# Read-and-gate kernel on one core: products of states and w_in for two slices at a time, state reads written in pairs, and the slots of the attention steps set anew

## The chip, the cores and the metric

The kernel runs on one core of one Trainium2 chip. The metric is the device time of one execution in microseconds (us). Of 13 runs of the kernel before, the median is 235.89 us (235.24 to 241.19). One execution was also recorded by the hardware profiler. Its trace gives the start and the length of every instruction and of every transfer; the page sums it up.

The names of the engines are those of the profile: PE is TensorE's matmuls, PEld its weight loads, DVE is VectorE, ACT is ScalarE, POOL is GpSimd, SP is SyncE, which here only issues transfers.

## What is computed

There are 8 batches of 8 heads with 512 tokens x and 32 states each, 64 wide. Tokens read from states and states read from tokens, both by softmax attention. The 544 rows of a batch (512 token reads, then 32 state reads, all heads side by side, 512 columns) go through a two-layer network of inner width 2048 with the activation "snake". From the reference:

```python
scores = scale * np.matmul(x, state.transpose(0, 1, 3, 2))   # a: softmax over the states
xread = np.matmul(a, state)
scores2 = scale * np.matmul(state, x.transpose(0, 1, 3, 2))  # a2: softmax over the tokens
sread = np.matmul(a2, x)
...
h = x @ w_in
s = np.sin(alpha * h)
g = h + s * s / (alpha + 1e-09)
return (g @ w_out).astype(np.float32)
```

The output has 8 × 544 = 4352 rows of 512 f32.

## The kernel before

**Two halves.** The large part is the network. The 4096 token rows are worked as 8 row tiles of 512, one for each batch (t = 0 to 7), and the 8 × 32 = 256 state rows are a ninth tile (t = 8). The inner width 2048 is worked in 16 slots f of 128 columns. So the main loop has 9 × 16 slots, and slot numbers in the tables count on through the tiles.

**One slot.** mm1(t,f) (L380) makes a 128x512 tile of h transposed in a "h" tile of PSUM (4 buffers), with two matmuls (L385). For token rows the product is not states times attention and then w_in: the states of the batch are multiplied with w_in first, which gives M (L353, m_step), and mm1 multiplies M with the attention AT. For the last tile mm1 takes w_in and the state reads xs_all directly (L391). ScalarE makes the sine (L397). Its square is made by POOL (L402) or, for the slots in table SQ, by VectorE (L409). Two slots later VectorE makes gT = h + square / alpha (L412, snake), which frees the h tile. Last come matmuls of mm2 (L421): each adds one 128-wide slice of gT times w_out to a 128x512 output tile in an "o" tile of PSUM (2 buffers). How many of them a slot has is in the tables TWO0, TWO1 and TWO, counted over the 64 of the row tile before (4 row groups of 128 rows, 16 slices each). A finished row group is copied by ScalarE (L427) and stored by SyncE (L433).

**The attention of the next batches** is put between by the table BATCH, in slots counted from the start of the tile before the batch's own ("P", "T", "S", "X", "R", "N", "A", "L") or from its own start ("W", "M"). Entry 3 holds for batches 3 to 7. The steps of a batch:

- L: POOL issues the load of x (L143; f32 in memory, bf16 on chip), through the same queue in which it computes its squares.
- P: two copies of VectorE pack x by token and head (L239, xp).
- T: transpose of xp, by TensorE and a VectorE copy for batches 0 and 1, from batch 2 by one transposing transfer that SyncE issues (L260).
- S: scores, two groups g of eight small matmuls (L276), into a "px" tile of PSUM each (2 buffers). X: the exponent on ScalarE (L285), which frees it; before it and after it ScalarE loads another table.
- R: sums and reciprocals (L289, L290); N: normalizing (L297 for g = 0, L300 for g = 1), on VectorE for the g in table ND, otherwise on POOL; A: transpose of the attention, AT, from batch 2 by a transfer (L266).
- W, Cs: the state reads and their sums over the tokens (L321, L332). Then xs: a reciprocal (L341) and two multiplications (L344) write the 32 state reads of the batch into xs_all.
- M: m_step (L353), one for each of four 512-column slices of w_in: eight matmuls of 32 columns in the array (L366, 64*32 in the profile) into two px tiles, then two copies to SBUF, each on ScalarE (L375) or VectorE (L377) as MA says.

**xs_all** is [P, Q, Ns, B]: for a head pair q and a state j the 8 batches lie next to each other. One batch writes single bf16 elements 16 bytes apart.

**What sets the order.** The schedule is written out by hand: the order of instructions on each engine is that in which the loop issues them, and a slot does its steps in this order:

```python
cur = mm1(t, f)
for fn, args in pe.get(t * FT + f, []): fn(*args)      # T, S, W, Cs, AT_, m_step
pend.append((t, f) + cur)
if len(pend) > LAG: snake(*pend.pop(0))                # LAG = 2
if due: squares()
for args in two.get(t * FT + f, []): mm2(*args)
for fn, args in post.get(t * FT + f, []): fn(*args)    # L, P, T_dma, X, R, N, AT_dma, xs
```

An instruction that waits holds up all behind it on its engine. SyncE's queue holds the stores and the transposing transfers; POOL's the loads of x and of the weights (L166 w_in, L169 w_out, in the order LOADS) beside its squares and normalizing.

**Start and end.** Before the loop, batch 0 is loaded, transposed and scored, with dummy matmuls between (warm_up, table WARM). After the loop the two row groups of the last tile are multiplied and stored; mm2_last (L440) does the second in halves.

Of the kernel before, what the change touches and what calls it, by code (L numbers as in the profile page):

```python
# [12 lines left out]
BF16 = mybir.dt.bfloat16  # L13
FP32 = mybir.dt.float32
# [5 lines left out]

BATCH = {0: {'M': (-11, 0, 6, 8), 'MA': ((1, 0), (1, 1), (1, 0), (1, 1))},
 1: {'P': (0, 1),
     'T': (3, 3),
     'S': (3, 3),
     'X': (3, 3),
     'R': (3, 7),
     'N': (8, 10),
     'A': 13,  # L30
     'M': (-6, 0, 3, 9),
     'MA': ((1, 1), (1, 1), (1, 1), (0, 1)),
     'W': (5, 5)},
 2: {'L': -8,
     'P': (-1, -1),
     'T': 1,
     'S': (6, 6),
     'X': (6, 6),
     'R': (7, 8),
     'N': (7, 11),  # L40
     'A': 11,
     'M': (-5, -2, 5, 10),
     'MA': ((1, 1), (1, 1), (1, 1), (0, 1)),
     'W': (-1, -1)},
 3: {'L': -18,
     'P': (-12, -11),
     'T': -6,
     'S': (2, 2),
     'X': (2, 2),
     'R': (3, 4),  # L50
     'N': (3, 9),
     'A': 12,
     'M': (-3, 1, 6, 8),
     'MA': ((1, 0), (1, 0), (0, 1), (1, 1)),
     'W': (-2, -2)}}

SQ = {0: (4, 8, 9, 11, 12, 15),
 1: (3, 6, 11, 12, 14),
 2: (0, 2, 5, 10, 11, 14),
 7: (0, 1, 2, 3, 4, 5, 8, 10, 12),  # L60
 8: (0, 1, 2, 3, 4, 8, 9, 11, 12, 14)}
ND = {1: (), 2: (0,), 3: (0,)}
XS0 = 0

TWO0 = (0, 0, 0, 0, 0, 4, 3, 1, 0, 0, 1, 6, 1, 2, 3, 0)
TWO1 = (2, 4, 2, 1, 1, 2, 3, 2, 5, 3, 9, 3, 0, 3, 3, 0)
TWO = (7, 3, 4, 7, 0, 6, 11, 5, 4, 1, 0, 6, 2, 4, 1, 3)
WARM = (9, 2, 1, 1)
LATER = 6

LOADS = ('i0', 'i1', 'x1', 'i2', 'o0', 'o1', 'i3', 'o2', 'o3')


@with_exitstack
def kernel(
# [9 lines left out]
    nc = tc.nc  # L85

    B, H, S, D = x.shape
    Ns = state.shape[2]
    P = nc.NUM_PARTITIONS
    C = S // P  # L90
    Q = H // 2
    G = 2
    HH = H // G
    TB = S + Ns
    DFF = moe_w_in.shape[1]
    FT = DFF // P
    FS = 4
    FW = DFF // FS
# [3 lines left out]
    const = ctx.enter_context(tc.tile_pool(name="const", bufs=1))  # L102
# [10 lines left out]
    psH = ctx.enter_context(tc.tile_pool(name="psH", bufs=4, space=bass.MemoryType.PSUM))  # L113
    psO = ctx.enter_context(tc.tile_pool(name="psO", bufs=2, space=bass.MemoryType.PSUM))
    psX = ctx.enter_context(tc.tile_pool(name="psX", bufs=2, space=bass.MemoryType.PSUM))
# [39 lines left out]
    w_in_sb = wpool.tile([P, Q, DFF], BF16, name="w_in_sb")  # L155
# [24 lines left out]
    stT = const.tile([P, B * G, P], BF16, name="stT")  # L180
    nc.vector.memset(stT[:].bitcast(U32), 0)
    alpha_sb = const.tile([P, FT], FP32, name="alpha_sb")
    inva_sb = const.tile([P, FT], FP32, name="inva_sb")
    xs_all = const.tile([P, Q, Ns, B], BF16, name="xs_all")

    def warm_up(n):
        if n:
            wp = psO.tile([P, S], FP32, name="o_ps", tag="o")
        for _ in range(n):
            nc.tensor.matmul(wp[:], warm[:, 0:P], warm[:], start=True, stop=True)  # L190
# [32 lines left out]
    class Att:  # L223
# [81 lines left out]
                    ALU.mult,  # L305
                )

        def AT_(a, gs, copy=nc.vector.tensor_copy):
            tp = psX.tile([P, len(gs), S], BF16, name="a_ps", tag="px")
            for k, g in enumerate(gs):  # L310
                for i in range(C):
                    nc.tensor.transpose(
                        tp[:, k, i * P:(i + 1) * P], a.A[:, g, i], ident[:]
                    )
            copy(a.AT[:, gs[0]:gs[-1] + 1, :], tp[:])

        def W(a, pool=psX, tag="px"):
            a.wc = pool.tile([P, Q, 3 * Ns], FP32, name="w_ps", tag=tag)
# [20 lines left out]
        def xs(a):  # L339
            rC = smallp.tile([P, Q, Ns], FP32, name="rC")  # L340
            nc.vector.reciprocal(rC[:], a.wc[:, :, 2 * Ns:])  # L341
            for r in range(2):
                rows = slice(r * D, (r + 1) * D)
                nc.vector.tensor_tensor(  # L344
                    xs_all[rows, :, :, a.b],
                    a.wc[rows, :, r * Ns:(r + 1) * Ns],
                    rC[rows],
                    ALU.mult,
                )

    def m_step(b, fs, on_act):  # L353
        if fs == 0:
            Ms[b] = mpool.tile([P, G, DFF], BF16, name="M")
        if b == 0 and fs == 0:
            mp = [psH.tile([P, FW], FP32, name="m0_ps", tag="h") for _ in range(G)]
        else:
            mp = [psX.tile([P, FW], FP32, name="m_ps", tag="px") for _ in range(G)]
        for h in range(2):  # L360
            for g in range(G):
                for r in range(2):
                    rows = slice(r * D, (r + 1) * D)
                    c0 = h * 2 * Ns + r * Ns
                    o0 = h * 2 * Ns + (r ^ g) * Ns
                    nc.tensor.matmul(  # L366
                        mp[g][o0:o0 + Ns, :],
                        stT[rows, b * G + g, c0:c0 + Ns],
                        w_in_sb[rows, 2 * g + h, fs * FW:(fs + 1) * FW],
                        start=True, stop=True,  # L370
                    )
        for g in range(G):
            dst = Ms[b][:, g, fs * FW:(fs + 1) * FW]
            if on_act[g]:
                nc.scalar.copy(dst, mp[g][:])  # L375
            else:
                nc.vector.tensor_copy(dst, mp[g][:])  # L377


    def mm1(t, f):  # L380
        n = S if t < B else B * Ns
        hp = psH.tile([P, S], FP32, name="h_ps", tag="h")
        if t < B:
            for g in range(G):
                nc.tensor.matmul(  # L385
                    hp[:, :n], Ms[t][:, g, f * P:(f + 1) * P], atts[t].AT[:, g, :],
                    start=(g == 0), stop=(g == G - 1),
                )
        else:
            for q in range(Q):  # L390
                nc.tensor.matmul(  # L391
                    hp[:, :n], w_in_sb[:, q, f * P:(f + 1) * P],
                    xs_all[:, q].rearrange("p j b -> p (j b)"),
                    start=(q == 0), stop=(q == Q - 1),
                )
        s = sinp.tile([P, S], BF16, name="s")
        nc.scalar.activation(s[:, :n], hp[:, :n], ACT.Sin, scale=alpha_sb[:, f:f + 1])  # L397
        s2 = sinp.tile([P, S], BF16, name="s2")
        if f in SQ[kind(t)]:
            late.append((s2, s, n))  # L400
        else:
            nc.gpsimd.tensor_tensor(s2[:, :n], s[:, :n], s[:, :n], ALU.mult)  # L402
        return hp, s2, n
# [26 lines left out]
    def store(t, st, o_sb, cols, eng):  # L430
        if t < B:
            r0 = t * TB + st
            eng.dma_start(out[r0:r0 + C * (P - 1) + 1:C, cols], o_sb[:, cols])  # L433
        else:
            r0 = S + st * P // B
            ov = out.rearrange("(b t) c -> t b c", t=TB)
            eng.dma_start(ov[r0:r0 + P // B, :, cols], o_sb[:, cols])


    def mm2_last(t, st):  # L440
# [23 lines left out]
    a = atts[0] = Att(0)  # L464
# [13 lines left out]
        load(*w)  # L478
    a.Rs(1)
    a.N(1, nc.vector)  # L480
    m_step(0, 0, (True, True))
    a.W(psO, "o")
    a.Cs()
    warm_up(WARM[3])
    nc.scalar.activation(tiny[:, 1:2], warm[:, 0:1], ACT.Sin)
    a.AT_([0], nc.scalar.copy)
    a.AT_([1])
    nc.vector.tensor_scalar(inva_sb[:], alpha_sb[:], 1e-9, None, op0=ALU.add)
    nc.vector.reciprocal(inva_sb[:], inva_sb[:])
# [5 lines left out]
    def add(d, s, fn, *args):  # L495
        d.setdefault(s, []).append((fn, args))
# [8 lines left out]
    for b in range(B):  # L505
        p = BATCH[min(b, 3)]
        s0 = (b - 1) * FT
        if b > 1:
            add(post, s0 + p["L"], load_x, b, 1)
        if b:  # L510
            add(post, s0 + p["P"][0], first, b)
            for g in range(G):
                add(post, s0 + p["P"][g], att, b, "pack", g)
            if b == 1:
                for g in range(G):
                    add(pe, s0 + p["T"][g], att, b, "T", g)
            else:
                add(post, s0 + p["T"], att, b, "T_dma")
            for g in range(G):
                add(pe, s0 + p["S"][g], att, b, "S", g)  # L520
                add(post, s0 + p["X"][g], att, b, "X", g)
                add(post, s0 + p["R"][g], att, b, "Rs", g)
                eng = nc.vector if g in ND[min(b, 3)] else nc.gpsimd
                add(post, s0 + p["N"][g], att, b, "N", g, eng)
            if b == 1:
                add(pe, s0 + p["A"], att, b, "AT_", [0, 1])
            else:
                add(post, s0 + p["A"], att, b, "AT_dma")
        s0 = b * FT
        if b:  # L530
            add(pe, s0 + p["W"][0], att, b, "W")
            add(pe, s0 + p["W"][1], att, b, "Cs")
        add(post, s0 + (p["W"][1] if b else XS0), att, b, "xs")
        for k in range(0 if b else 1, FS):
            add(pe, s0 + p["M"][k], m_step, b, k, p["MA"][k])

    def rows(t, counts, todo):
        for f, c in enumerate(counts):
# [65 lines left out]
```

## Time and profile before

| | |
|---|---|
| median of 13 runs | 235.89 us |
| the profiled execution | 235.61 us |
| its span, first to last instruction | 233.8 us |
| mean granted TensorE clock | 0.993 |
| instructions | 4190 |
| VectorE copies of M (L377) | x18, 685 ns each |
| ScalarE copies of M (L375) | x46, 590 ns each |
| products of states and w_in (L366) | x256 matmuls, 64*32 |
| stores (L433, L437) | x35, 2.2 to 2.3 us to landing |
| transposing transfers of x and of A | x6 and x6, 3.9 and 3.0 us to landing |

Of the 235.61 us some 1.8 lie around the span. In the lists of groups, a row has the line, the engine, the operation, the tiles out<-in, the shapes, how often it occurs, then busy time and mean duration, then the idle time of the engine just ahead of it and what ended that. In a timeline, a row has the start, the duration, and in brackets how long the engine was idle before, with the releaser. Matmuls overlap in the array, so the busy times of rows in TensorE's timeline overlap at their edges; a 128x512 matmul's own record is longer than the time by which it moves the stream on.

Where x's tiles come from and when: x of batch 1 was issued at 6.94 us and took 10.17 to land, that of batch 2 was issued at 28.94 and took 7.44.

### The profile page before, as it was taken

The page shows a single profiled execution, that of the slowest core. Times are in us where ns is not written, and L with a number is a line of the kernel's source. Part 1 is how long each engine was busy: PE and PEld are TensorE (multiplying, and loading weights), DVE is VectorE, ACT ScalarE, POOL GpSimd, SP SyncE. Part 2 cuts the span into 40 slices and gives each one's busy share as a digit, 9 for nine tenths or more (in the row PEclk, how much of TensorE's full clock was granted, in tenths as well). Part 3 has the DMA queues.
Part 4 walks back from the last instruction along what each step waited for, and adds up shares of the span by engine and source line. Part 5 has one row for each costly group of instructions (what it writes and reads, how often), then busy time and mean ns, then how long its engine had stood idle before and what let it go on. Part 6 is the DMA issues. An engine that isn't in the chain of part 4 may idle for free.

```text
span 233.8 us, 4190 instructions
## 1 busy us (share of the span) xinstructions
PE 219.3 (94%) x1534; PEld 103.4 (44%) x1534; DVE 184.0 (79%) x314; ACT 163.6 (70%) x265; POOL 109.0 (47%) x116
## 2 busy tenths in 40 slices
PE   7767897799999999999999999999998999999993
PEld 3524242444544444444444443444444434565652
DVE  3779898998996999879996999699959976654500
ACT  4787975997696769775978597859776666544420
POOL 3875777446336732674167417641565033512110
PEclk9997999999999999999999999999999999999999
DMA  6999998607811780278026912440212011111113
GB/s 222 193 197 206 206 142 107 171 3 181 135 45 47 179 135 3 90 178 133 7 91 90 182 45 93 110 114 4 90 45 77 15 49 62 72 46 46 45 48 90
DMA packets 36613, 23.35 MB, mean 100 GB/s; under 512 B 19680, under 2 KB 32240, under 8 KB 36592
## 3 DMA queue, kind: packets, MB, share of 16 engines
q0 software_dynamic: 11504, 7.87, 23.9%
q1 hardware_dynamic: 25056, 15.21, 22.2%
q8 instruction: 12, 0.20, 0.3%
q14 instruction: 9, 0.07, 0.1%
q10 hardware_dynamic: 32, 0.01, 0.0%
HBM read 17.31 MB, written 8.91 MB: 112 GB/s over the span
## 4 chain that ended last, share of the span: by engine, by line
PE 72%; DMA 12%; DVE 7%; POOL 3%; issue 2%; ACT 2%; ACTq 0%; POOLq 0%
PE o_ps L421 44%; PE h_ps L385 18%; DMA xnat<-in_x_dram 8%; PE m_ps L366 3%; PE h_ps L391 3%; DVE gT L412 2%; DVE xs_all L344 2%; PE s_ps L276 2%; DMA st_nat<-in_state_dram 2%; POOL s L402 1%; DMA AT<-A 1%; DMA out_dram<-o_sb 1%; DVE rC L341 1%; DVE xp L239 1%; PE w_ps L321 1%
## 5 line engine op out<-in xcount | busy, mean ns | idle before, releaser
L402 POOL TENSOR_TENSOR s<-s 128x512 bf16<-128x512 bf16 (+1 forms) x84 | 85.8, 1027 | 109.6 <-ACT s L397 104.7
L421 PE MATMUL o_ps<-w_out_sb,gT 128*128 128x512 bf16 x528 | 134.9, 380 | 0.0
L397 ACT ACTIVATE s<-h_ps,alpha_sb 128x512 bf16<-128x512 f32 (+1 forms) x144 | 93.7, 669 | 52.0 <-PE h_ps L385 37.0
L412 DVE SCALAR_TENSOR_TENSOR gT<-s,inva_sb,h_ps 128x512 bf16<-128x512 bf16 (+1 forms) x144 | 99.4, 712 | 20.9 <-POOL s L402 19.7
L385 PE MATMUL h_ps<-AT,M 128*128 128x512 bf16 x256 | 75.0, 383 | 3.6 <-DVE gT L412 2.3
L421 PEld LDWEIGHTS <-gT 128*128 128x128 bf16 x528 | 49.1, 98 | 57.4 <-issue 6.9
L385 PEld LDWEIGHTS <-M 128*128 128x128 bf16 x256 | 24.7, 98 | 34.9 <-issue 7.9
L409 DVE TENSOR_TENSOR s<-s 128x512 bf16<-128x512 bf16 (+1 forms) x60 | 25.2, 429 | 6.5 <-ACT s L397 5.9
L375 ACT CAST M<-m_ps 128x512 bf16<-128x512 f32 x46 | 25.5, 590 | 0.4 <-PE m_ps L366 0.4
L427 ACT COPY o_sb<-o_ps 128x512 f32<-128x512 f32 x33 | 19.5, 592 | 4.9 <-PE o_ps L421 4.7
L377 DVE CAST M<-m_ps 128x512 bf16<-128x512 f32 x18 | 12.3, 685 | 2.1 <-PE m_ps L366 1.9
L366 PE MATMUL m_ps<-w_in_sb,stT 64*32 64x512 bf16 x256 | 13.1, 387 | 0.8 <-DMA w_in_sb<-in_moe_w_in_dram 0.8
L289 DVE TENSOR_REDUCE R<-E 128x16 f32<-128x512 bf16 x16 | 10.8, 678 | 1.8 <-ACT E L285 1.6
L344 DVE TENSOR_TENSOR xs_all<-w_ps,rC 64x128 bf16<-64x128 f32 x16 | 11.6, 728 | 0.4
L239 DVE COPY xp<-xnat 128x1024 bf16<-128x1024 bf16 x14 | 9.5, 688 | 1.5 <-DMA xnat<-in_x_dram 1.5
L285 ACT ACTIVATE E<-s_ps 128x512 bf16<-128x512 f32 x16 | 8.9, 595 | 2.2 <-PE s_ps L276 2.0
L366 PEld LDWEIGHTS <-stT 64*32 64x32 bf16 x256 | 3.7, 89 | 14.1 <-issue 13.1
L391 PE MATMUL h_ps<-xs_all,w_in_sb 128*128 128x256 bf16 x64 | 9.6, 273 | 0.0
L397 ACT ACT_TABLE_LOAD x7 | 9.0, 1283 | 0.4 <-PE h_ps L385 0.3
L285 ACT ACT_TABLE_LOAD x7 | 9.0, 1283 | 0.1
L341 DVE RECIPROCAL rC<-w_ps 128x128 f32<-128x128 f32 x8 | 7.6, 949 | 1.0 <-PE w_ps L332 1.0
L276 PE MATMUL s_ps<-stT,xT 128*128 128x64 bf16 x128 | 6.0, 200 | 2.3 <-DVE xs_all L344 1.2
(53 smaller groups left out, 99.1 us busy)
## 6 DMA issues: line engine op xcount, KB each, us to landing
out_dram<-o_sb SPq DMA_DIRECT2D x33, 256.0 KB, 2.3
xnat<-in_x_dram POOLq DMA_DIRECT2D x7, 512.0 KB, 7.4
w_in_sb<-in_moe_w_in_dram POOLq DMA_DIRECT2D x4, 512.0 KB, 9.4
w_out_sb<-in_moe_w_out_dram POOLq DMA_DIRECT2D x4, 512.0 KB, 16.0
x_first<-in_x_dram SPq DMA_DIRECT2D x2, 512.0 KB, 5.2
st_nat<-in_state_dram SPq DMA_DIRECT2D x1, 512.0 KB, 3.7
out_dram<-o_sb SPq DMA_DIRECT2D x2, 128.0 KB, 2.2
xT<-xp SPq DMA_TRANSPOSE x6, 3.9
```

Of the source, the lines that this page charges most:

```text
L285: nc.scalar.activation(a.E[:, g], a.sp[g][:], ACT.Exp, scale=scale)
L344: nc.vector.tensor_tensor(xs_all[rows, :, :, a.b], a.wc[rows, :, r * Ns:(r + 1) * Ns], rC[rows], ALU.mult,)
L366: nc.tensor.matmul(mp[g][o0:o0 + Ns, :], stT[rows, b * G + g, c0:c0 + Ns], w_in_sb[rows, 2 * g + h, fs * FW:(fs + 1) * FW], start=True, st ...
L375: nc.scalar.copy(dst, mp[g][:])
L385: nc.tensor.matmul(hp[:, :n], Ms[t][:, g, f * P:(f + 1) * P], atts[t].AT[:, g, :], start=(g == 0), stop=(g == G - 1),)
L391: nc.tensor.matmul(hp[:, :n], w_in_sb[:, q, f * P:(f + 1) * P], xs_all[:, q].rearrange("p j b -> p (j b)"), start=(q == 0), stop=(q == Q - 1),
L397: nc.scalar.activation(s[:, :n], hp[:, :n], ACT.Sin, scale=alpha_sb[:, f:f + 1])
L402: nc.gpsimd.tensor_tensor(s2[:, :n], s[:, :n], s[:, :n], ALU.mult)
L409: nc.vector.tensor_tensor(s2[:, :n], s[:, :n], s[:, :n], ALU.mult)
L412: nc.vector.scalar_tensor_tensor(gT[t][:, f, :n], s2[:, :n], inva_sb[:, f:f + 1], hp[:, :n], ALU.mult, ALU.add)
L421: nc.tensor.matmul(op[:], gT[t][:, ft, st * P:(st + 1) * P], w_out_sb[:, ft, :], start=(ft == 0), stop=(ft == FT - 1),)
L427: nc.scalar.copy(o_sb[:], op[:])
```

## The change

1. **Pairs of slices.** m_step takes a tuple of slices. For batches 2 to 7 (SLICES) it does two slices at once: sixteen matmuls in a row, the first slice into an o and an h tile, the second into two px tiles, and then four copies. Batches 0 and 1 keep single slices, and slice 0 of batch 0 uses px tiles instead of h tiles.
2. **State reads in pairs.** xs_all becomes [P, Q, B/4, Ns/2, 4, 2]: a batch writes two neighbouring elements at a time. This changes the order of rows in the last tile, and each store of that tile becomes two of 64 rows, one issued by SyncE and one by ScalarE.
3. **AT_** (batches 0 and 1): both copies are on VectorE; the first of batch 0 was on ScalarE.
4. **Tables.** x of batch 2 is loaded 8 slots earlier; its pack and its transpose come 2 to 4 slots later. For batches 3 to 7 the load is one slot later, the first pack one earlier, the transpose two earlier, S of group 0 two earlier, normalizing, A and the products M at other slots, and group 1 instead of group 0 is normalized by VectorE. The slots squared by VectorE go from 6, 5, 6, 9, 10 (tiles 0, 1, 2 to 6, 7, 8) to 10, 9, 5, 7, 6. The counts of mm2 per slot, the dummy matmuls and the order of the weight loads are changed too.

```diff
- 2: {'L': -8,
-     'P': (-1, -1),
-     'T': 1,
+ 2: {'L': -16,
+     'P': (1, 3),
+     'T': 5,
      'S': (6, 6),
...
- 3: {'L': -18,
-     'P': (-12, -11),
-     'T': -6,
-     'S': (2, 2),
+ 3: {'L': -17,
+     'P': (-13, -11),
+     'T': -8,
+     'S': (0, 2),
      'X': (2, 2),
-     'R': (3, 4),
-     'N': (3, 9),
-     'A': 12,
-     'M': (-3, 1, 6, 8),
-     'MA': ((1, 0), (1, 0), (0, 1), (1, 1)),
+     'R': (5, 8),
+     'N': (9, 12),
+     'A': 14,
+     'M': (-4, -3, 4, 4),
+     'MA': ((0, 1), (1, 1), (0, 1), (1, 0)),
      'W': (-2, -2)}}
...
+SLICES = {0: ((0,), (1,), (2,), (3,)), 1: ((0,), (1,), (2,), (3,)), 2: ((0, 1), (2, 3)), 3: ((0, 1), (2, 3))}
...
-TWO0 = (0, 0, 0, 0, 0, 4, 3, 1, 0, 0, 1, 6, 1, 2, 3, 0)
-TWO1 = (2, 4, 2, 1, 1, 2, 3, 2, 5, 3, 9, 3, 0, 3, 3, 0)
-TWO = (7, 3, 4, 7, 0, 6, 11, 5, 4, 1, 0, 6, 2, 4, 1, 3)
-WARM = (9, 2, 1, 1)
+TWO0 = (0, 0, 0, 1, 2, 0, 2, 0, 2, 0, 0, 6, 1, 1, 6, 1)
+TWO1 = (2, 3, 5, 1, 3, 0, 5, 2, 3, 2, 3, 5, 1, 6, 1, 0)
+TWO = (1, 2, 6, 3, 10, 5, 3, 3, 4, 3, 5, 0, 5, 4, 4, 6)
+WARM = (7, 1, 2, 2, 0, 1, 2)
...
-LOADS = ('i0', 'i1', 'x1', 'i2', 'o0', 'o1', 'i3', 'o2', 'o3')
+LOADS = ('i0', 'i1', 'x1', 'o0', 'i2', 'i3', 'o1', 'o2', 'o3')
...
-    xs_all = const.tile([P, Q, Ns, B], BF16, name="xs_all")
+    xs_all = const.tile([P, Q, B // 4, Ns // 2, 4, 2], BF16, name="xs_all")
...
-                    xs_all[rows, :, :, a.b],
-                    a.wc[rows, :, r * Ns:(r + 1) * Ns],
-                    rC[rows],
+                    xs_all[rows, :, a.b // 4, :, a.b % 4, :],
+                    a.wc[rows, :, r * Ns:(r + 1) * Ns].rearrange("p q (k l) -> p q k l", l=2),
+                    rC[rows].rearrange("p q (k l) -> p q k l", l=2),
...
-            copy(a.AT[:, gs[0]:gs[-1] + 1, :], tp[:])
+            nc.vector.tensor_copy(a.AT[:, gs[0]:gs[-1] + 1, :], tp[:])
...
+        homes = [(psX, "px"), (psX, "px")]
+        if len(slices) == 2:
+            homes = [(psO, "o"), (psH, "h")] + homes
+        mp = {}
+        for k, (pool, tag) in enumerate(homes):
+            mp[slices[k // G], k % G] = pool.tile([P, FW], FP32, name="m_ps", tag=tag)
+        for fs in slices:
+            for h in range(2):
+                for g in range(G):
+                    for r in range(2):
...
-            r0 = S + st * P // B
-            ov = out.rearrange("(b t) c -> t b c", t=TB)
-            eng.dma_start(ov[r0:r0 + P // B, :, cols], o_sb[:, cols])
+            ov = out.rearrange("(b t) c -> b t c", t=TB)[st * 4:(st + 1) * 4, S:, cols]
+            for l, e in ((0, eng), (1, nc.scalar)):
+                e.dma_start(ov[:, l::2].rearrange("b k c -> k b c"), o_sb[l::2, cols])
```

## The prediction

> **What bounds the kernel now.** I read the page's busy table and slices first, then the chain that ended last.
>
> ```profile
> PE 219.3 (94%) x1534; PEld 103.4 (44%) x1534; DVE 184.0 (79%) x314; ACT 163.6 (70%) x265; POOL 109.0 (47%) x116
> PEclk9997999999999999999999999999999999999999
> PE 72%; DMA 12%; DVE 7%; POOL 3%; issue 2%; ACT 2%; ACTq 0%; POOLq 0%
> ```
>
> TensorE is the bound, at full clock but for one slice near 20 us. The 14.5 us in which it is not busy hold the start (x and state landings, part of the DMA's 12%), the last store, and a few stalls. By stage, from the answer on windows:
>
> ```profile
> 14.00:46.00 32.00, 25.96 (x201) 11.34 (x201) 29.13 (x48) 25.42 (x42) 20.35 (x20) 0.95 1.05 171
> 82.80:106.90 24.10, 24.10 (x170) 10.79 (x169) 21.35 (x36) 18.46 (x30) 12.47 (x12) 1.00 0.46 100
> 179.00:201.00 22.00, 21.36 (x118) 9.07 (x117) 17.78 (x31) 14.50 (x24) 6.38 (x7) 1.00 0.13 48
> ```
>
> Columns: stretch, length, busy PE, PEld, DVE, ACT, POOL. A steady row tile (82.8 to 106.9) has PE busy throughout and VectorE 89%: there only less TensorE time or a new stall moves the end. From 14 to 46 us PE lacks 6.0 us while VectorE is 91% busy: there VectorE and the loads set the pace. Now TensorE's own timeline, around one product of states and w_in (L366):
>
> ```profile
> 92.30 0.59 PE L385 MATMUL h_ps<-AT,M 128*128 128x512 bf16 x2
> 92.82 0.41 PE L366 MATMUL m_ps<-w_in_sb,stT 64*32 64x512 bf16 x8
> 93.17 1.04 PE L421 MATMUL o_ps<-w_out_sb,gT 128*128 128x512 bf16 x4
> ```
>
> A 512-column matmul takes 0.216 us of the stream (11 in 2.37 us elsewhere in the chain). The pair of L385 ends its stream at 92.30 + 0.43 = 92.73; L421 starts at 93.17. So one m_step costs PE 0.44: 0.09 before its first matmul, about 0.03 for the eight to start beside one another, 0.32 until the next full-size matmul streams.
>
> The stalls in VectorE's, TensorE's and SyncE's timelines:
>
> ```profile
> 36.40 1.82 DVE L239 COPY xp<-xnat 128x1024 bf16<-128x1024 bf16 x2 [0.82 <-DMA xnat<-in_x_dram]
> 178.92 1.47 DVE L344 TENSOR_TENSOR xs_all<-w_ps,rC 64x128 bf16<-64x128 f32 x2
> ```
> ```profile
> 38.94 0.59 PE L385 MATMUL h_ps<-AT,M 128*128 128x512 bf16 x2 [1.20 <-DVE gT L412]
> 45.95 0.41 PE L276 MATMUL s_ps<-stT,xT 128*128 128x64 bf16 x8 [1.22 <-DVE xs_all L344]
> 181.23 0.59 PE L385 MATMUL h_ps<-AT,M 128*128 128x512 bf16 x2 [0.64 <-DVE gT L412]
> ```
> ```profile
> 125.16 2.97 SPq L260 DMA_TRANSPOSE xT<-xp  x1
> ```
>
> VectorE, stuck on batch 2's pack, lets PE stand 1.20 us; xs (L341, L344: 0.96 + 1.47) lets it stand 1.22 and 0.64. At 131 us the transpose of x was late, A's transpose behind it landed at 131.14, and mm1(5,0) started at 131.18, some 0.7 late (that tile's period was 24.32 against 23.8 to 24.05). The answer on x's tiles gives the loads:
>
> ```profile
> DMA to landing us min/median/max: 5.9/7.4/10.2
> ```
>
> **What the Trainium skill says.** Four places of the Trainium skill bear on this. "TensorEngine Tiling (Array Packing)", Key Properties: a change of tiling mode drains TensorE. The trace agrees: the 0.09 and 0.32 around the 64*32 matmuls. "SBUF — State Buffer", Specifications: lines of 16 bytes, two hits on a line wanted for full rate. In xs_all an element lies 16 bytes from the next: L344 takes 728 ns for 128 elements a partition, L412 712 for 512. Pairs are not in this trace. "DMA: Bandwidth & Descriptors", Issuing engines are not separate DMA queues: transfers from different engines share the same 16. Agrees: the transpose of x took 3.17 us at 38.25 beside x3's load, about 1.5 undisturbed. "TensorE: Matmul & The Clock Gate", Part 3: a weight load overlaps running matmuls only when it goes to another row group. This speaks against a free second wave in the pair; the trace has no sixteen of these in a row.
>
> **The change part by part.** Against the profiled execution, 235.61 (span 233.8 and 1.8 around it), 0.28 under the median of 235.89.
>
> *Pairs of slices.* Batches 2 to 7 have 24 single m_steps, 24 × 0.436 = 10.5 us; these become 12 of sixteen matmuls. A pair costs 0.09 in, 0.03, a second wave, 0.32 out. If the wave streams on, it adds one matmul's 0.216: 0.65, which saves 0.22 each, 2.6 in all. If the second wave waits for the first to drain, 0.78: saves 0.09 each, 1.1. No saving at all would need a full drain and fresh entry between the waves, which nothing in one mode asks for. I take 2.6, since the L332 products, also in a smaller mode and on one tile, follow each other at their stream rate of about 55 ns with weight loads between. PE per tile is then 23.86 − 2 × 0.22 = 23.43. The copies to SBUF (0.59 on ScalarE, 0.69 on VectorE) stay 4 per pair.
>
> *Start and batch 2.* x2's load goes from slot 8 to slot 0, its pack from slot 15 to 17 and 19, its transpose from 17 to 21. In before it was issued at 28.94 and landed at 36.38, and VectorE stood. Issued some 8 slots earlier it lands before its pack; xp no longer blocks VectorE: −1.36 at 37.4. But i2 goes behind o0 (loads land 2.54 us apart) and its product moves from slot 6 with it; the start up to 17.11 stays, as x1 still lands then (issued 6.94, 10.17 long). x3's load no longer overlaps the transpose, now issued near 40.5 behind two stores and landing 3.85 to 5.4 later (before: 53.02 to 56.85 and 38.25 to 43.65), 44.3 to 45.9, beside S, which reads it then. AT_'s first copy goes from ScalarE (0.57) to VectorE (0.42), −0.1. VectorE, the bound here, gets four more squares in each of the first two tiles, 8 × 0.42, which POOL (1.03 each) had in parallel. Followed by hand through both instruction orders with the durations above, the first S comes 0.6 earlier (fewer products ahead of it on PE), mm1(1,0) 0.5, the end of batch 2's S at 45.1 to 45.5 with three more matmuls of L421 done against 46.2 (1.3 ahead), and mm1(2,0), with Cs (0.33) now behind xs's former place, at 57.8 instead of 59.02: −1.2. Bounds −2.5 (every one of the listed stalls) and +0.5 (the transpose late by 1.6 and VectorE full).
>
> *xs in pairs.* Two elements a line: I take L344 at about 0.4, between 0.31 (L412's rate) and 0.73 (none). Two per batch, −0.65 on VectorE. On the path it is the stall at 181: −0.7; steady tiles hide the rest behind PE. With the late transpose at 131 partly gone, as S moves from slot 2 to 0/2 and T two slots earlier, −0.3. Together −1.0; bounds −1.7 and 0.
>
> *Last tile's stores.* Eight 64-row stores in two queues for four: issue 0.54 each on SP, and ScalarE has little after 226 us. The end runs PE 229.9, copy 0.42, issue 230.39, landing 232.62: the same. 0; −0.1 to +0.3.
>
> *New waits.* The pair's second slice uses the px slots that the exps of S free: the wave at slot 4 can wait about 0.1, with mm1(5) queued behind it on PE; 5 tiles, 0.5. The pair's first tile sits in an o slot: the next row group's first L421 waits for its copy (0.69, on VectorE behind the pack), with all later PE work queued behind it; three to ten matmuls (0.6 to 2.2) stand ahead and cover it. At slot 12 the h slot wants snake(t,9) just behind mm1(12), since slot 11 has no mm2; 0.1 in all. A's transpose stands behind store(t−1,2) on SyncE and lands about when mm1(t+1,0) wants it; 0 (bound 1.5). Sum +0.6.
>
> *x loads 4 to 7.* Slot 14 becomes 15, packs at 20 and 21 become 19 and 21. The load stands on POOL behind the square of slot 14, 1.8 after mm1(14); from there to mm1(19) PE has W and Cs (0.94), a pair of mm1 (0.43) and 23 matmuls (4.97), and VectorE gets to the pack 1.2 later: 7.6 − 1.8 = 5.8 us. VectorE holds about 1.0 before PE lacks gT. So latency over 6.8 stalls PE. In before they took 6.24, 5.86, 8.25 and 7.5: 0, 0, 1.45, 0.7 = 2.15, of which about 0.5 covers the waits above: +1.6. Bounds 0 and 7.3.
>
> Sum: −2.6 − 1.2 − 1.0 + 0.6 + 1.6 = −2.6: 235.61 − 2.6 = 233.0.
>
> **The rivals.**
> *Clean:* the loads land in time, nothing stalls for them: −4.2, 231.4. For it: two of four loads took 6.2 or less. Against: the median is 7.4.
> *Serial pairs:* the second wave drains the first: 1.5 less saved, 234.5. For it: the page on TensorE above; against: L332.
> *Slower: VectorE held by the pack.* Place: pack g0 at slot 19, ahead of the snakes and M copies on VectorE. With the shifted load every latency is as 8.25, beside stores and A's transpose: 5 × 1.45 = 7.3, less the gains of 4.2: +3.1, 238.7. It decides from a mean latency of 7.6 (5 × 0.84 = 4.2). For: at 113.29 and 136.59 it was near or past. Against: the same load has 5.9 beside the same traffic.
> *No change:* waits of tight buffers use up the gain, about 235.6.
>
> **How the numbers follow.** Forecast 233.0 (232.2 to 234.6) 0.45; clean 0.25; serial 0.10; slower 0.12; no change 0.08. The range 231.0 to 235.6 takes in the first three, and the bounds of the pairs and the start, and leaves out slower. A measurement here tells 0.2%, 0.47 us, from no change. Faster: 0.45 + 0.25 + 0.10 = 0.80; same 0.08; slower 0.12.
>
> **What would show it.** Sixteen L366 matmuls in 0.65 between full-size ones (0.78: serial). L344 near 0.4 us. No VectorE idle by x at 36; mm1(2,0) near 57.8. Periods of mm1(t,0) near 23.5, and where longer, VectorE idle before L239 by the x load with PE's wait on gT behind it. No wait of 0.6 at 181. It is wrong if L239 waits in every tile, if PE waits at slots 4 and 12 for more than 0.3, or if mm1(2,0) comes after 59.

## The result, and the profile after

The changed kernel took 231.13 us (median of 11 runs, 230.47 to 232.09). The ratio to the kernel before is 0.9786, with a 95% interval of 0.9757 to 0.9815: about 5.0 us less. The prediction was 233.0 (231.0 to 235.6). Of the kernel before 48 runs have a median of 237.71: many of them ran at a lower granted clock and took up to 8 us more, and the ratio leaves disturbed ones out; none of the changed kernel's runs had a clock below 0.996. The profiled execution took 231.44 (span 229.7) against 235.61 (233.8), so the traces below account for 4.2 us.

Line numbers have moved: L366 is now L373 (product of states and w_in), L385 is L393 (mm1), L421 is L429 (mm2), L344 is L347 (xs), L412 is L420 (snake), L266 is L269 (transpose of A), L409 and L402 are L417 and L410 (squares), L427 and L433 are L435 and L441 (copy and store of a row group), L239 is L242 (pack), L276 is L279 (S); L385 is now VectorE's copy of M. The busy table, the clock row and the shares of the chain that ended last, of the page after:

```profile
PE 214.3 (93%) x1536; PEld 102.3 (45%) x1536; DVE 170.8 (74%) x309; ACT 164.4 (72%) x266; POOL 111.4 (49%) x120
PEclk9999999999999999999999999999999999999999
PE 72%; DMA 13%; ACT 7%; issue 2%; DVE 2%; POOL 1%; SPq 0%; ACTq 0%
```

PE has 5.0 us less to do and VectorE 13.2 less. VectorE fell from 7% of the chain to 2%. PE's share of the span still did not rise: something else waits. TensorE's timeline after, around a pair of slices, and the row of xs in the answer on its tile (minimum, median, maximum in ns):

```profile
72.16 1.03 PE L393 MATMUL h_ps<-AT,M 128*128 128x512 bf16 x4
73.12 0.63 PE L373 MATMUL m_ps<-w_in_sb,stT 64*32 64x512 bf16 x16
73.68 1.25 PE L429 MATMUL o_ps<-w_out_sb,gT 128*128 128x512 bf16 x5
```
```profile
L347 DVE TENSOR_TENSOR xs_all<-w_ps,rC x16: 282/289/295, 15.3 to 173.6; 64x128 bf16<-64x128 f32 x16
```

Four matmuls of L393 stream 0.86 us from 72.16, to 73.03; L429 streams at 73.68. The pair costs 0.65, as forecast. xs takes 0.29, not 0.73. Two rows from TensorE's timelines after show what waits now:

```profile
104.38 0.60 PE L393 MATMUL h_ps<-AT,M 128*128 128x512 bf16 x2 [0.74 <-DMA AT<-A]
176.41 0.61 PE L393 MATMUL h_ps<-AT,M 128*128 128x512 bf16 x2 [1.45 <-DMA AT<-A]
```

The first mm1 of tiles 4 and 7 waits for the transposed attention. The brackets count from the end of the matmul before it, whose record overlaps; by the starts of the matmuls, as waits of PE are given below where no row is shown, the two are 0.91 and 1.61. In the chain of waits after, ahead of the first of them (start, length, what):

```profile
98.90 0.64 ACT o_sb L435
...
99.55 0.33 SPq L441
...
100.05 4.28 DMA AT<-A
...
104.38 0.60 PE h_ps L393 x2
```

A's transpose is issued behind the store (L441), which waits for ScalarE's copy; and then it takes 4.28 us where other tiles have 2.7. Where the 4.2 us went, by the first sine of each row tile:

| first sine of tile | 0 | 1 | 2 | 3 | 4 | 5 | 6 | 7 | 8 |
|---|---|---|---|---|---|---|---|---|---|
| before | 14.87 | 35.61 | 59.66 | 83.51 | 107.55 | 131.88 | 155.78 | 179.82 | 202.67 |
| after | 14.62 | 34.57 | 56.18 | 80.69 | 105.08 | 128.55 | 152.02 | 177.11 | 198.48 |
| a_at11, below | 15.21 | 34.69 | 56.45 | 80.97 | 104.44 | 127.91 | 151.38 | 174.85 | 196.22 |

At tile 2 the changed kernel is 3.5 ahead, of which 0.43 is Cs, moved behind that point. From tile 2 to tile 8 it gains only 0.7 more, though the shortest period of a steady tile fell from 23.85 to 23.47: tiles 2, 3 and 6 take 24.51, 24.39 and 25.09. From tile 8 to the end both take 31.2.

### The profile page after: what moved, and what is told of

Same layout as the page of the kernel before. It is cut to its first block, busy times and chain, and to the rows that moved or that the text cites. A ratio compares the mean times of both kernels' runs of the same rounds, so it can differ in the third digit from the quotient of the medians.

```text
span 229.7 us, 4214 instructions
## 1 busy us (share of the span) xinstructions
PE 214.3 (93%) x1536; PEld 102.3 (45%) x1536; DVE 170.8 (74%) x309; ACT 164.4 (72%) x266; POOL 111.4 (49%) x120
## 4 chain that ended last, share of the span: by engine, by line
PE 72%; DMA 13%; ACT 7%; issue 2%; DVE 2%; POOL 1%; SPq 0%; ACTq 0%
PE o_ps L429 43%; PE h_ps L393 20%; DMA xnat<-in_x_dram 5%; DMA AT<-A 4%; PE h_ps L399 3%; PE m_ps L373 3%; ACT s L405 3%; ACT M L383 2%; DMA xT<-xp 2%; DMA st_nat<-in_state_dram 2%; PE s_ps L279 1%; DMA out_dram<-o_sb 1%; ACT o_sb L435 1%; PE w_ps L324 1%; POOL w_in_sb L168 1%
## 5 line engine op out<-in xcount | busy, mean ns | idle before, releaser
L429 PE MATMUL o_ps<-w_out_sb,gT 128*128 128x512 bf16 x528 | 135.5, 380 | 0.0
L410 POOL TENSOR_TENSOR s<-s 128x512 bf16<-128x512 bf16 (+1 forms) x87 | 87.4, 1014 | 98.9 <-ACT s L405 78.9
L420 DVE SCALAR_TENSOR_TENSOR gT<-s,inva_sb,h_ps 128x512 bf16<-128x512 bf16 (+1 forms) x144 | 99.6, 708 | 23.6 <-POOL s L410 22.3
L393 PE MATMUL h_ps<-AT,M 128*128 128x512 bf16 x256 | 75.2, 380 | 2.9 <-DMA AT<-A 2.2
L429 PEld LDWEIGHTS <-gT 128*128 128x128 bf16 x528 | 49.5, 98 | 57.4 <-issue 5.2
L393 PEld LDWEIGHTS <-M 128*128 128x128 bf16 x256 | 24.5, 98 | 32.7 <-DMA AT<-A 3.2
L417 DVE TENSOR_TENSOR s<-s 128x512 bf16<-128x512 bf16 (+1 forms) x57 | 24.5, 436 | 5.5 <-ACT s L405 4.6
L435 ACT COPY o_sb<-o_ps 128x512 f32<-128x512 f32 x33 | 19.5, 594 | 7.7 <-PE o_ps L429 7.3
L385 DVE CAST M<-m_ps 128x512 bf16<-128x512 f32 x16 | 10.6, 688 | 9.4 <-PE m_ps L373 9.4
L373 PE MATMUL m_ps<-w_in_sb,stT 64*32 64x512 bf16 x256 | 11.3, 383 | 1.4 <-ACT o_sb L435 0.6
L300 POOL TENSOR_TENSOR A<-E,rR 128x512 bf16<-128x512 bf16 x8 | 8.4, 1047 | 5.2 <-DVE rR L293 5.2
L242 DVE COPY xp<-xnat 128x1024 bf16<-128x1024 bf16 x14 | 5.6, 412 | 3.8 <-DMA xnat<-in_x_dram 3.8
L279 PE MATMUL s_ps<-stT,xT 128*128 128x64 bf16 x128 | 6.2, 194 | 2.1 <-DMA xT<-xp 1.5
L399 PEld LDWEIGHTS <-w_in_sb 128*128 128x128 bf16 x64 | 6.3, 98 | 4.1
L373 PEld LDWEIGHTS <-stT 64*32 64x32 bf16 x256 | 3.2, 89 | 10.8 <-issue 8.9
```

The lines of the kernel that those rows point to most:

```text
L373: nc.tensor.matmul(mp[fs, g][o0:o0 + Ns, :], stT[rows, b * G + g, c0:c0 + Ns], w_in_sb[rows, 2 * g + h, fs * FW:(fs + 1) * FW], start=True ...
L393: nc.tensor.matmul(hp[:, :n], Ms[t][:, g, f * P:(f + 1) * P], atts[t].AT[:, g, :], start=(g == 0), stop=(g == G - 1),)
L399: nc.tensor.matmul(hp[:, :n], w_in_sb[:, q, f * P:(f + 1) * P], xs_all[:, q].rearrange("p h k b l -> p (h k b l)"), start=(q == 0), stop=( ...
L417: nc.vector.tensor_tensor(s2[:, :n], s[:, :n], s[:, :n], ALU.mult)
L420: nc.vector.scalar_tensor_tensor(gT[t][:, f, :n], s2[:, :n], inva_sb[:, f:f + 1], hp[:, :n], ALU.mult, ALU.add)
L429: nc.tensor.matmul(op[:], gT[t][:, ft, st * P:(st + 1) * P], w_out_sb[:, ft, :], start=(ft == 0), stop=(ft == FT - 1),)
```

## The experiments

Times are medians. The kernels named a_ start from the changed kernel (231.13; 231.36 when run again beside three of them), those named b_ from the kernel before.

**a_single: the pairs undone.**

```diff
-3: ((0, 1), (2, 3))        # and 2:
+3: ((0,), (1,), (2,), (3,))
-     'M': (-3, 1, 5, 7),
+     'M': (-4, -3, 5, 7),
...
-     'M': (-4, -3, 4, 4),
+     'M': (-4, -3, 4, 6),
```

> The changed kernel with single slices again for batches 2 to 7 (slots -4, -3, 5, 7 for batch 2 and -4, -3, 4, 6 from batch 3; same copies). Theory (pairs save 2 x 0.435 - 0.651 = 0.22 us of TensorE each, and TensorE is the bound): +2.4 us for 12 pairs, and about 24 groups of eight matmuls at 0.435 in the trace. Rival (a later stall, the wait for A's transpose, swallows what the pairs save): under +1.0.

Measured 233.44, +2.3, near the forecast of +2.4, but as the difference of two larger terms, some +4.5 and −2.5 in the profiled executions. Where the changed kernel has no wait (tiles 4 and 5), periods are 24.14 instead of 23.47. These 0.67 are more than the 2 × 0.22 of the pairs' own cost: the first of two products at slot 4 lasts longer, where in a pair only 0.04 is lost. TensorE's timeline of a_single, where a product undisturbed has 0.41:

```profile
111.11 0.67 PE L373 MATMUL m_ps<-w_in_sb,stT 64*32 64x512 bf16 x8
```

Its third matmul starts 0.26 late, released by the second of the exps of S, which holds a px tile until then (it ends at 111.32); a pair puts its first slice into other tiles. On the other side, no mm1 waits for AT here: tiles 3 and 6 last 24.1 as well, against 24.39 and 25.09. So the rival is right in part: of what the pairs save, the wait for A's transpose swallows some in the changed kernel.

**a_xsold and b_xs: xs in the old layout in the changed kernel, in the new one in the kernel before.**

```diff
-xs_all = const.tile([P, Q, B // 4, Ns // 2, 4, 2], BF16, name="xs_all")
+xs_all = const.tile([P, Q, Ns, B], BF16, name="xs_all")
```

(with the views and the stores of the last tile that belong to it; b_xs is the reverse)

> The changed kernel with the old xs_all (single elements 16 bytes apart) and the old stores of the last tile. L344's two multiplications go back from 2 x 0.29 to 2 x 0.73, +0.88 us of VectorE per batch. Theory (steady tiles hide it behind TensorE): +0.2, at most +0.7, with xs's successor late once in the last tiles. Rival (VectorE's queue is on the path in each tile): +3 or more, with TensorE waits on gT behind L344 in most tiles.

> The kernel before with the new xs_all and the new stores of the last tile alone. Theory: L344 0.29 instead of 0.73 us, and PE's wait of 0.8 at 181 goes, the 1.4 us at 45 (S of batch 2 group 1 behind xs) shrinks by up to 0.9, others are hidden: -1.0 to -1.7 against the kernel before. Rival (VectorE is the pace everywhere): -3 or more; or its place is taken by the next wait: 0 to -0.5.

a_xsold took 232.44, +1.3: more than expected, far less than the rival. Its L347 is at 726 ns again, and TensorE's timeline has a new wait of 0.93:

```profile
59.73 0.41 PE L279 MATMUL s_ps<-stT,xT 128*128 128x64 bf16 x8 [0.93 <-DVE xs_all L347]
```

By the first sines this wait costs little: tile 2 lasts only 0.15 longer, and the 0.75 that PE waits for ScalarE's copy of an o tile in the changed kernel (64.42 us) is gone. In the profiled executions the loss is 0.84, and it is there at the start of tile 2 (57.02 instead of 56.18); what it is made of was not separated.

b_xs took 233.34, ratio 0.9888 (0.9864 to 0.9913): about −2.6, again more than expected, and about half of what the whole change brings. Its tile 2 starts 1.2 earlier than that of the kernel before: the wait of S for xs, 1.22 in the prediction's row, has shrunk.

```profile
44.73 0.41 PE L276 MATMUL s_ps<-stT,xT 128*128 128x64 bf16 x8 [0.33 <-DVE xs_all L344]
```

Its tile 7 lasts 22.04 instead of 22.85: the wait at 181 us is gone. Gone too are PE's waits of 0.35 at 62 us and of 0.16 in each of tiles 3, 4 and 6. So steady tiles did not hide all of xs: most of its cost lay in two places, and a little in most tiles. The two kernels price it differently; one reason is seen in tile 2 of the changed one, above.

**a_at11: A's transpose ahead of the store.**

```diff
-     'N': (9, 12),
-     'A': 14,
+     'N': (9, 11),
+     'A': 11,
```

> The changed kernel with A's transpose for batches 3 to 7 at slot 11 (normalizing of group 1 at 11 instead of 12), so that it stands ahead of the store of row group 2 on SyncE. Theory (AT is late because it waits behind that store, whose copy waits behind three copies of M on ScalarE): AT is issued about 1 us earlier, the waits of mm1(t,0) on AT (0.9 and 1.6 in the profile after) are gone, -1.5 to -2.5. Rival (the transfers are late by themselves, 4.3 and 5.0 us instead of 2.7): waits remain, within 0.5 of the changed kernel.

> The kernel a_at11 once more, on the same chip as the changed kernel: 2.3 below it. If the gain of a_at11 was that of another chip, under 1.

Measured 228.81, and 229.01 beside the changed kernel's 231.36 on one chip: −2.35. Its ratio to the kernel before was 0.9697 (0.9659 to 0.9734). The transpose of batch 4 is now issued at 97.46 instead of 100.05, lands at 100.2, and mm1(4,0) does not wait. SyncE's queue in a_at11, with the store (L441) behind the transpose:

```profile
97.46 1.23 SPq L269 DMA_TRANSPOSE AT<-A  x1
99.83 0.33 SPq L441 DMA_DIRECT2D out_dram<-o_sb  x1
```

The last row of the table above has periods of 23.47 in all tiles from 3 to 6. This version is faster than both kernels.

> The changed kernel once more, beside a_at11_again, a_l8 and a_l16 on one chip: 231.1, with AT of batches 4 and 7 again over 4 us (the instruction packets fall where they fell), 2.7 for the others.

The changed kernel run again took 231.36, and AT of batches 4 and 7 made PE wait 0.76 and 1.67: the lateness is no chance of one run.

**a_shift: why just batches 4 and 7.** In the answer on transfers for 99 to 105 us of the changed kernel, where AT is late, and for 147.5 to 151, where it is not (for a queue: packets, MB, share of time; for an issue: median us to landing):

```profile
q8 instruction: 1, 0.02, 1.5%
...
AT<-A SPq DMA_TRANSPOSE x1, 4.3
```
```profile
AT<-A SPq DMA_TRANSPOSE x1, 2.7
```

The second stretch has no instruction packet. In the whole trace there are twelve packets of 16 KB, which would be one for each 256 of the 3072 matmuls and weight loads on the page. So TensorE's instruction stream was moved, with nothing else changed in the loop:

```diff
-    warm_up(WARM[0])
+    warm_up(3, 22)              # 22 matmuls of 64 columns for 4 of 512
...
-add(pe, s0 + p["T"][0], warm_up, WARM[5])
+add(pe, s0 + p["T"][0], warm_up, WARM[5], 26)
```

> The changed kernel with 44 dummy matmuls more ahead of the work of tile 0 (48 of 64 columns for 4 of 512; at the very start and in the wait for x1), which moves TensorE's later instructions 88 places on in its stream; the loop is unchanged. In the traces AT of batches 4 and 7 takes 4.3 and 5.0 us where a 16 KB packet of the instruction queue falls into it (101.2 and 173.6 us in the profile after), and 2.7 where none does. Theory (the fetch of TensorE's own instructions holds the transfer up): the packets fall some 9.5 us earlier, about 92 and 164; AT of batches 4 and 7 lands in 2.7; the two waits of mm1(t,0), 0.9 and 1.6, are gone, -1.5 to -2.5 against the changed kernel (231.1) less what the dummies cost at the start (up to 1). Rival (the place in the loop or the buffer makes these two late): they take over 4 again, no gain.

Time 233.36: no gain, as the rival said of the time. But its mechanism is refuted. AT of batches 4 and 7 now lands in 2.7 and makes nobody wait; that of batches 3 and 6, which was on time, takes 4.4 and 4.6, and PE waits 1.0 and 1.3 for it. Transfers of a_shift from 149.5 to 154.8 us (batch 6) and from 174.2 to 178 (batch 7):

```profile
q8 instruction: 1, 0.02, 2.0%
...
AT<-A SPq DMA_TRANSPOSE x1, 4.6
```
```profile
AT<-A SPq DMA_TRANSPOSE x1, 2.7
```

The lateness moved with the packets. After the first one the packets came 1.0 to 6.8 us earlier, not 9.5 as I had worked out, and fell onto other transfers. Another now lies beside x's load for batch 4: the pack waits 2.86 (2.08 in the changed kernel) and PE 1.19 behind it. That and the wait for batch 3's AT make tile 2 last 27.07 us instead of 24.51, and batch 6's makes tile 5 last 24.75; tiles 3 and 6 are back at 23.47, so what was won there is lost here. In every kernel on record that starts from the changed one, A's transposes from batch 2 on take 2.7 to 2.8 us or have such a packet in them. The fetch delays; a place without any collision was not found this way. Issuing the transpose earlier (a_at11) makes the delay harmless: there batch 5's takes 3.6 with a packet in it, and nobody waits. So the waits need both, the late place behind the store and the packet.

**b_x2 and a_l8: the load of batch 2 alone.** b_x2 moves it to slot 0 in the kernel before, a_l8 back to slot 8 in the changed one.

```diff
- 2: {'L': -8,
+ 2: {'L': -16,
```

> The kernel before with x of batch 2 loaded at slot 0 instead of 8, and nothing else. Theory (the late landing alone blocks VectorE at 36): VectorE's wait of 0.8 and PE's of 1.36 at 37 us go, -1.0 to -1.5. Rival (the 512 KB load then delays the weight loads beside it, or the transpose of x that waits on the same engines): between -0.5 and +1.

> The changed kernel with x of batch 2 loaded at slot 8 as before, packs and transpose where the change put them. Theory (the later pack and transpose, after x of batch 3 has landed, are what helps; the earlier load adds little): issued near 27 it lands near 34 to 36, just before the pack at 36.2; within 0.5 of the changed kernel. Rival (the earlier load is needed): x of batch 2 and 3 overlap, the pack or the transpose is late and S of batch 2 waits over 3 us, +1.5 or more.

b_x2 was slower, ratio 1.0173 (1.0130 to 1.0215), some +4. PE's wait of 1.36 at 37 us is gone, but the transpose of x runs into batch 3's load. From the answer on the transpose's tile, TensorE's and VectorE's timelines of b_x2:

```profile
DMA to landing us min/median/max: 3.8/3.9/9.4
```
```profile
47.07 0.41 PE L276 MATMUL s_ps<-stT,xT 128*128 128x64 bf16 x8 [2.51 <-DMA xT<-xp]
```
```profile
44.91 0.78 DVE L239 COPY xp<-xnat 128x1024 bf16<-128x1024 bf16 x1 [2.35 <-DMA xnat<-in_x_dram]
```

The load was issued at 36.94, the transpose at 37.65. The transpose took 9.4 us and the load was late too. A clock of 0.979 to 0.986 in these runs adds to it: the run at 0.986 took 239.18, while runs of the kernel before with 0.985 or 0.986 took 236.65 to 237.36, so some 2 of the 4 are left for the edit. In the changed kernel the load of batch 3 is issued at 33.13 and the transpose not before 39.26, so they meet no more: the earlier load, which costs when moved alone, needs the later transpose.

a_l8 took 234.95, +3.6 (+2.6 in the two profiled executions, both at full clock), and neither theory had the cause right. The load lands in time, and S of batch 2 waits 1.68, as in the changed kernel (1.70). But issuing it occupies POOL at 27.29, inside tile 0. POOL's and VectorE's timelines of a_l8, and TensorE's:

```profile
27.29 0.95 POOL L145 DMA_DIRECT2D xnat<-in_x_dram  x1
28.26 1.06 POOL L303 TENSOR_TENSOR A<-E,rR 128x512 bf16<-128x512 bf16 x1
29.27 1.04 POOL L410 TENSOR_TENSOR s<-s 128x512 bf16<-128x512 bf16 x1
30.27 1.04 POOL L300 TENSOR_TENSOR A<-E,rR 128x512 bf16<-128x512 bf16 x1
```
```profile
28.05 3.89 DVE L417 TENSOR_TENSOR s<-s 128x512 bf16<-128x512 bf16 x2
```
```profile
32.65 0.59 PE L393 MATMUL h_ps<-AT,M 128*128 128x512 bf16 x2 [2.50 <-DVE gT L420]
```

Of the two squares of VectorE, 0.42 each elsewhere, the first lasts from 28.05 to 31.60: POOL does three operations without a break meanwhile, and the square ends 0.29 after the last of them. Then snake is late and PE waits 2.5 for an h tile. The Trainium skill ("SBUF — State Buffer", Terms, shared port pair) says that VectorE and GpSimd hold one pair of ports exclusively, the loser blocking fully. The traces agree, though no run was made to test it: in those of before, after, a_l8, a_single, a_at11 and b_x2, 44 squares of VectorE (512 columns) begin inside a square or a normalizing of POOL, and 40 of them end 0.28 to 0.29 us after it; the other four begin in its last 0.1 us and take their usual 0.42.

**a_l16: x loads of batches 3 to 7 one slot later.**

```diff
- 3: {'L': -17,
+ 3: {'L': -16,
```

> The changed kernel with the loads of x for batches 3 to 7 one slot later (slot 16 instead of 15); the packs stay. In the profile after, x is issued some 6.3 us before its pack, lands 5.7 to 6.7 after the issue, VectorE waits 0.5 and PE not at all. Theory (VectorE has about 1 us in hand there): about 1 us later VectorE waits 1.5 before the first pack and PE 0.5 to 1.0 in each of five tiles, +2 to +5. Rival (the x loads have room to spare): no PE wait, within 0.3 of the changed kernel.

Measured 252.41 (248.97 to 254.81), +21, and +18 and +19 in the two shorter executions: the theory's way, about four times the upper end of its range. Slot 15's square is VectorE's, slot 16's POOL's, so on POOL the load moved two squares on: from its issue to VectorE's arrival at the pack there are 2.8 us (88.26 to 91.05) instead of 5.8 (78.50 to 84.28). The granted clock, 0.96 to 0.98 in these runs, adds to it: in the trace it is one half for 13.7 us in three stretches, which begin within, at the end of and 1.2 us behind a wait of PE of over 3 us, and so it accounts for at most 6.8 of the +19. VectorE's and TensorE's timelines of a_l16:

```profile
94.13 1.18 DVE L242 COPY xp<-xnat 128x1024 bf16<-128x1024 bf16 x1 [3.08 <-DMA xnat<-in_x_dram]
95.24 1.27 DVE L385 CAST M<-m_ps 128x512 bf16<-128x512 f32 x2
```
```profile
95.97 1.24 PE L429 MATMUL o_ps<-w_out_sb,gT 128*128 128x512 bf16 x5 [3.20 <-DVE M L385]
```

This is the chain of the prediction's slower rival: pack ahead of the copy of M on VectorE, the copy ahead of the o tile that the next row group needs, and PE standing 3.2 us in the tile. What sets it off differs: the loads land in 5.8 to 6.0 us, not 8.25, but are issued too late.

**a_warm0: without the three new dummy matmuls of tile 0.**

```diff
-WARM = (7, 1, 2, 2, 0, 1, 2)
+WARM = (7, 1, 2, 2, 0, 0, 0)
```

> The changed kernel without the three dummy matmuls ahead of batch 1's transposes and scores (slot 3 of tile 0). Theory (they keep TensorE's granted clock up over the wait for x1): the clock falls to half for some 3.4 us near 20 us as in the kernel before, +0.8. Rival (the change's other moves kept it up): clock 1.0 throughout, within 0.3.

Measured 231.92, +0.8 in the median, but the clock stayed at 1.0 in the profile: the size came, the reason given for it did not. The executions of the two kernels overlap (231.45 to 232.32, and 230.47 to 232.09). The first sine of tile 1 comes at 35.08, where the changed kernel has 34.57 and 34.50, but a_xsold and a_single, which keep these matmuls, 35.06 and 35.00; what the 0.8 is made of stays open.

**a_best: two more waits, tried on top of a_at11.**

```diff
-     'S': (6, 6), 'X': (6, 6), 'R': (6, 9),
+     'S': (7, 7), 'X': (7, 7), 'R': (7, 9),
...
-     'M': (-3, 1, 5, 7), 'MA': ((0, 1), (1, 1), (1, 1), (1, 1)),
+     'M': (-3, 1, 4, 7), 'MA': ((0, 1), (1, 1), (0, 1), (1, 0)),
```

> The kernel a_at11 with batch 2's scores one slot later (slot 7 instead of 6) and with batch 2's second pair at slot 4 instead of 5, copies as from batch 3. Theory: S of batch 2 waits 1.7 to 1.8 us for the transpose of x at slot 6, one slot (1.5 us) later it waits 0.3, and the work in between fills it; the pair at slot 5 waits 0.75 for ScalarE's copy of an o tile, at slot 4 that tile is free: -1.5 to -2.2 against a_at11 (228.8), so 226.6 to 227.3. Rival (VectorE and ScalarE set the pace up to 60 us, the waits only move): within 0.5 of a_at11.

Measured 230.84, 2.0 slower than a_at11: further off than the rival's 0.5. The waits moved, as the rival said: S of batch 2 waits only 0.2, but PE then waits 1.2 and 0.5 for gT, and in tile 2 it waits for VectorE's copy of M, where it had waited 0.75 for ScalarE:

```profile
66.78 1.46 PE L429 MATMUL o_ps<-w_out_sb,gT 128*128 128x512 bf16 x6 [1.61 <-DVE M L385]
```

Tiles 1 to 3 together last 1.5 longer than in a_at11. The profiled execution, 232.48, is 1.6 longer than the other three, and its first sine comes at 17.28, 2 us later than in a_at11; that is no part of this. Here neither wait was removed by moving the instruction that showed it; which of the two moves cost what was not separated.

## Why the prediction was right, and where its terms were off

| term | predicted | in the trace after |
|---|---|---|
| 12 pairs | −2.6 | −2.5 |
| start, up to mm1(2,0), without its pair | −1.2 | −2.8 |
| stalls of steady tiles that go | −1.0 | −1.9 |
| new waits at slots 4, 5 and 12 | +0.6 | +0.7 |
| AT behind the store | 0 (bound 1.5) | +2.5 |
| x loads 4 to 7 | +1.6 | 0 |
| end | 0 | 0 |
| sum | −2.6 | −4.0 of 4.2 |

*Pairs.* Right: the trace shows the cost that was forecast. The second wave streams on: a pair costs 0.65 (0.69 where it waits 0.04 for the exps), against two of 0.436. The serial rival, 0.78, is out: in most pairs all weight loads of the second eight start 25 to 50 ns after the first matmul, on the row groups on which the first eight still stream. What the prediction named as speaking against a free second wave does not hold in this trace. a_single's total agrees, but not for this reason alone (above).

*The start.* The most mis-sized of the gains, outside its own bounds (−2.5 to +0.5). Counted in the traces, both kernels had started nearly as many full-size matmuls by 28 us (28 and 29), but 67 and 79 by 40 us. Most of the lead arises where VectorE held PE up in the kernel before: waits of 0.23, 1.36 and 0.44 at 34, 37 and 39 us, by the starts of its matmuls, of which none is left. I had counted the 1.36 and given most of the rest away to four more squares per tile on VectorE and to late weights, neither of which showed. Part of the start belongs to xs: the layout alone brings tile 2 forward by 1.2 in the kernel before (b_xs), and undoing it puts it back by 0.8 in the changed one (a_xsold). What AT_'s copies and the order of the weight loads bring was not tried. That S of batch 2 would meet its transpose was right: it waits 1.7. The half-clock slice near 20 us mattered less than it looked: executions of the kernel before at clock 1.0 took 235.65 and 235.89, the profiled one at 0.993 235.61.

*xs.* Estimated at 0.4, measured 0.29, below even the 0.31 put down to L412's rate (712 ns for 512 elements, which is 0.18 in proportion; the fixed part that makes it 0.31 is not shown). b_xs shows the layout alone to be worth about 2.6 in the kernel before, where the prediction had 0.7 on the path and the rest hidden behind PE in steady tiles. The stalls that went are 0.35 at 62 us, 0.28 at 131, 0.81 at 181 and three of 0.16: all but the one at 131 go in b_xs too. That one was read as 0.7 late in the prediction; PE's wait in it was 0.28.

*x loads.* The mechanism is real (a_l16) and the 5.8 us of cover were right; the latency was wrong: loads landed 5.7 to 6.7 after issue, not 5.9 to 8.25, and waits of VectorE of 2.1 and 0.6 ahead of the pack did not reach PE beyond the 0.7 counted at slot 5. Why two of these loads were slower in the kernel before was not tried; one of them had a 16 KB instruction packet beside it.

*A's transpose.* Named, then priced at nothing, from a trace in which the six took 2.7 to 3.2 us and no packet of instructions had fallen well inside one. It cost 2.5 in two tiles, and a_at11 won 2.35 back. Elsewhere it had 0.7 to spare (tile 5: issued 124.44, landed 2.7 later, mm1(5,0) at 127.86). This error of +2.5 and those of the x loads and the start, −1.6 each, and of the stalls, −0.9, cancel in part; with the start alone right, the sum would have come to 231.4. So that the measured time lies within the range is in part luck: it lies at the range's lower end, nearer to the clean rival's 231.4 than to 233.0, though that rival's reason, that nothing stalls, holds for the loads only.

*What should show it right or wrong.* The pairs, L347 and the wait at 181 came as forecast; mm1(2,0) came at 55.4, not 57.8; the period is 23.47 where nothing waits, as forecast. L242 waits for x in three of the five tiles, and PE waits 0.04 at slot 4 but 0.75 once at slot 5.

## What to carry to other kernels

Take the length of a wait-free transfer, and then ask what it stands behind in its issuing queue and what else runs on the same engines: a slot that leaves 0.7 us of room is none when a 4.3 us landing occurs. Move a load together with the transfers that it can meet; moved alone it cost some 2 to 4 us here, and in a queue that also computes one slot meant 3 us. Where a small product costs TensorE time in going in and out (here 0.44 for one), put two side by side (0.65) if PSUM has the tiles for it: this gain can be read from one timeline in advance; the waits for tiles that come or go with it cannot. And when one edit is undone, see which other waits go with it before its price is read off the total.

## What the runs showed of the hardware

- The traces list the fetch of instructions among the queues of the 16 DMA engines: a 16 KB packet took 0.9 to 1.8 us, and A's transposes with one well inside took 3.0 to 5.1 us instead of 2.7 (18 in eleven traces). In the kernel before, the transpose of x at 125.16, which held SyncE's queue for 2.97 instead of 1.5, also had one in it (125.5, 1.4 us).
- Sixteen 64*32 matmuls in a row: eight start within 25 ns, the next eight 203 ns later, and the exit costs 0.31. The weight loads of the second eight overlap the first eight, on the same row groups.
- VectorE writes 128 bf16 elements a partition in 289 ns when two lie side by side every 16 bytes, and in 726 ns when one does; the dense case is not in the traces.
- A square of VectorE that began inside an operation of POOL ended 0.28 us after it (40 of 44 in six traces); beside three back-to-back operations one of 0.42 us lasted 3.56.
- The transpose of x landed in 3.6 to 4.4 us with no load of x and no packet of instructions beside it, and in 5.4 (before), 6.0 (b_xs), 6.9 (a_l16) and 9.4 us (b_x2) beside a load of x.
